# First batch's activation: the raw first 256 columns kept two places further on, and split without copies

## The chip, the cores and the metric

The kernel runs on one core of a Trainium2 chip. A core has a matmul engine (TensorE; PE in the rows, its weight loads PEld), a vector engine (VectorE, DVE), a scalar engine (ScalarE, ACT), a general engine (GpSimd, POOL) and a queue that issues transfers (SyncE, SP). The metric is device time in microseconds (us) of one execution of the whole program; the time given for the kernel is the median of its runs.

## The reference

```python
B, H, S, D = 4, 12, 448, 64          # batches, heads, tokens, head size
q_n, k_n = rmsnorm(q, g_q), rmsnorm(k, g_k)
attn = softmax(q_n @ k_n.T / 8)       # per head
x = (attn @ v)                        # heads side by side: 1792 tokens x 768
h = x @ moe_w_in                      # 768 -> 2048
g = h / (1 + exp(-1.702 * h))
y = g @ moe_w_out                     # 2048 -> 768
h2 = y @ moe2_w_in                    # 768 -> 2048
out = (max(h2, 0) + alpha * min(h2, 0)) @ moe2_w_out
```

All is float32. The weights and the four batches of tokens are needed whole; no step depends on the order in which batches are done.

## The kernel before

TensorE multiplies float16 here. So each float32 operand is split in two float16 parts, a high one (`hi`, made by ScalarE) and a low one (`lo`, what is left, made by VectorE as `scalar_tensor_tensor` from the float32 source and `hi`): `split`, lines 137 to 142, whose two instructions show as L139 and L140. A product is three matmuls (hi·hi, hi·lo, lo·hi).

**The stages.** Attention of batch 0 runs first, beside the unpacking of the two weight matrices of the first MoE layer. Its second half is interleaved with the first 256 token columns of batch 0's first matmul, because these are ready before the other 192. Then batch 0's remaining 192 columns, its activation and its second matmul (`first_moe1`, `moe1_out`) run beside the attention of batch 1; `moe1(b)` of the later batches runs beside the attention of the batch after it; and the second MoE layer ends the kernel.

**The first layer of batch 0.** There are KF = 16 blocks of 128 hidden units, m = 0 to 15. For each block `first_in(cols, m, g, t)` issues 18 matmuls into a PSUM tile `hp` (profile line L720), then a tanh on ScalarE into an SBUF tile `t` (L731), then `(tanh + 1) * hp` on VectorE (L732). It is called twice for a block: with columns 0 to 255 during the attention of batch 0, and with columns 256 to 447 in `first_moe1`. PSUM tiles `hp` come from `ps_m`, which has three buffers; `t` comes from the pool `work`, tag "t", which has two, and it is the same tag that `split_g`, `moe1` and the output `y` use.

**Where the result lies.** The tile `g0` has 16 places, one for each block, each of 2 x 448 float16: room for the two parts of the block, or for 448 float32 words. In its first half a place that isn't split yet keeps the block's float32 result ("raw"). `unsplit(g, m)` is place m seen as float32. The first 256 words of each place hold the raw first columns; the remaining 192 words of the 16 places are the landing area of the second weight matrix (`raw1o`), until it is unpacked.

**How it is split before the change.** Both parts of block m go to place m, where its raw result lies as well, so that the raw words have to be out of the way first. For blocks 0 to 4 (RAW0 = 5) the last 192 columns are written raw beside the first 256, and then, once the scales of the second weight matrix are known, `split_g` copies each block's 448 words to a `t` tile (L809) and splits from there. For blocks 5 to 15 a `t` tile is taken first, the 256 raw words are copied into it (L751), `first_in` puts the other 192 columns beside them, and the split reads that tile:

```python
t = work.tile([128, S], F32, tag="t", name="t")
nc.vector.tensor_copy(out=t[:, 0:FIRST], in_=unsplit(g, m)[:, 0:FIRST])
first_in(slice(FIRST, S), m, g, t)
split((g[:, m, 0], g[:, m, 1]), t, scales["w1o"][1][:, m:m + 1])
```

**What sets the order.** Each engine works its instructions in a fixed order. That order is not the program's: a planner runs through the program with costs of its own and puts on each engine what is ready, earlier program text first. A pool tile is given out in program order, so that a later user of `work` "t" waits until both uses of an earlier one are over. In program text the attention of batch 1 (`other_batches`) is interleaved with `first_moe1` and `moe1_out` by ticks; `B1_AT = 24` ticks pass before its first unit, that is 12 blocks. A unit of the attention of batches 1 to 3 is: scores (L499, PSUM pool `ps_s`, two buffers), maximum (L504, DVE), exponent (L523, ACT), reciprocal and a high part (L562, L565), a low part (L592, DVE), a transposing DMA (L598, SP), and the product with v (L616). `normalize` and `prep_pair` ready q and k of a pair of heads (L395, L397, L417, L418, L451, L452; for some pairs L417, L418 and L452 run on POOL). `v_scale(b)` loads v of a batch in pieces to the tiles `vst` of `raw_p` (two buffers) and reduces them (L310, L311).

Of the kernel before, what the change touches and what calls it, by code (L numbers as in the profile page):

```python
# [9 lines left out]
F32 = mybir.dt.float32  # L10
# [4 lines left out]
ALU = mybir.AluOpType  # L15
# [5 lines left out]
RAW0 = 5  # L21
# [35 lines left out]
def attention_moe_kernel(  # L57
# [17 lines left out]
    nc = tc.nc  # L75
# [7 lines left out]
    KF = FF // 128  # L83
# [7 lines left out]
    work = ctx.enter_context(tc.tile_pool(name="work", bufs=2))  # L91
# [45 lines left out]
    def split(dst, src, scale):  # L137

        nc.scalar.activation(out=dst[0], in_=src, func=AF.Copy, scale=scale)  # L139
        nc.vector.scalar_tensor_tensor(  # L140
            out=dst[1], in0=src, scalar=scale, in1=dst[0], op0=ALU.mult, op1=ALU.subtract
        )
# [111 lines left out]
    def later_rows(w, d, other):  # L254

        nj = w.shape[1]
        return lambda j: w[:, j + d].rearrange("p e n -> p (e n)").bitcast(F32) if j + d < nj else other(j)

    scales = {}
    loads = {}  # L260
    w1i = big.tile([128, KD, 2, FF], F16, tag="w", name="w1i", bufs=2)
    w1o = big.tile([128, KF, 2, DM], F16, tag="w", name="w1o", bufs=2)
# [3 lines left out]
    raw_p = att.enter_context(tc.tile_pool(name="raw_p", bufs=2))  # L266
# [206 lines left out]
    FIRST = 256  # L473
# [236 lines left out]
    def urgent(on):  # L710
        return tc.high_priority(on) if on else ExitStack()

    def first_in(cols, m, g, t):

        n = cols.stop - cols.start
        ps = ps_m.tile([128, n], F32, tag="m", name="hp")
        i = 0
        for kk in range(KD):
            for e, f in ((0, 0), (0, 1), (1, 0)):
                nc.tensor.matmul(  # L720
                    out=ps, lhsT=w1i[:, kk, e, m * 128:(m + 1) * 128], rhs=xs[0, kk][:, f, cols], start=(i == 0),
                    stop=(i == 3 * KD - 1)
                )
                i += 1
        if t is None:
            t = work.tile([128, S], F32, tag="t", name="t")
            dst = unsplit(g, m)
        else:
            dst = t
        with urgent(HP0):  # L730
            nc.scalar.activation(out=t[:, cols], in_=ps, func=AF.Tanh, scale=c_t[:, 0:1])  # L731
            nc.vector.scalar_tensor_tensor(out=dst[:, cols], in0=t[:, cols], scalar=1.0, in1=ps, op0=ALU.add, op1=ALU.mult)  # L732

    def moe1_scales(b):
        nc.vector.tensor_scalar(
# [4 lines left out]
    def first_moe1(g):  # L740

        for m in range(KF):
            if m == RAW0:
                for _ in w1o_steps:
                    pass
                split_g(g, scales["w1o"][1], range(RAW0))
            if m < RAW0:
                first_in(slice(FIRST, S), m, g, None)
            else:
                t = work.tile([128, S], F32, tag="t", name="t")  # L750
                nc.vector.tensor_copy(out=t[:, 0:FIRST], in_=unsplit(g, m)[:, 0:FIRST])  # L751
                first_in(slice(FIRST, S), m, g, t)
                split((g[:, m, 0], g[:, m, 1]), t, scales["w1o"][1][:, m:m + 1])
            yield
            yield
        yield from moe1_out(0, g)
# [24 lines left out]
    def moe1_out(b, g):  # L781
        nc.vector.tensor_scalar(
            out=c_y[:, b:b + 1], in0=c_y[:, b:b + 1], scalar1=scales["w1o"][0], scalar2=2.0 ** 11, op0=ALU.mult, op1=ALU.mult
        )
        for j in range(KD):
            ps = ps_m.tile([128, S], F32, tag="m", name="yp")
            n = 0
            for m in range(KF):
                for e, f in ((0, 0), (0, 1), (1, 0)):
                    nc.tensor.matmul(  # L790
                        out=ps, lhsT=w1o[:, m, e, j * 128:(j + 1) * 128], rhs=g[:, m, f], start=(n == 0), stop=(n == 3 * KF - 1)
                    )
                    n += 1
                if m in (3, 7, 11):
                    yield
            y = work.tile([128, S], F32, tag="t", name="y")
            with urgent(HP2):
                nc.scalar.activation(out=y, in_=ps, func=AF.Copy, scale=c_y[:, b:b + 1])
            nc.sync.dma_start(out=y_dram[j * 128:(j + 1) * 128, b * S:(b + 1) * S], in_=y)
            yield  # L800

    def unsplit(g, m):

        return g[:, m].rearrange("p e t -> p (e t)").bitcast(F32)

    def split_g(g, sc, ms=range(KF)):
        for m in ms:
            t = work.tile([128, g.shape[3]], F32, tag="t", name="t")
            nc.vector.tensor_copy(out=t, in_=unsplit(g, m))  # L809
            split((g[:, m, 0], g[:, m, 1]), t, sc[:, m:m + 1])  # L810

    TICKS = 2 * KF + 4 * KD

# [330 lines left out]
    if True:  # L1144
# [18 lines left out]
        def num1o(j):  # L1163
# [8 lines left out]
        w1o_steps = weights(  # L1172
            moe_w_out, "w1o", lambda: w1o, later_rows(w1o, 2, num1o), lambda t: raw1o[:, 4 * (t % R1O):4 * (t % R1O) + 4], 2,
            R1O, 2.0 ** -25, scales, G1O
        )
# [21 lines left out]
        for i, _ in enumerate(steps):  # L1197
            pairs = max(0, (i - LAG + 1) // 2)
            rows = KF - 2 if pairs >= 4 else (HOLD + pairs * HELD) // (2 * DM) - 2
            while n1o < min(1 + 2 * rows + 3 * (rows // 2), (i + 1) * W1O_RATE, 57):  # L1200
                next(w1o_steps)
                n1o += 1
            if i >= M_AT and i - M_AT < KF:
                first_in(slice(0, FIRST), i - M_AT, g0, None)
            if i == VS_AT:
                with tc.issue_after(loads["w1i"][-1].ins):
                    v_scale(1)
# [15 lines left out]
        for b in range(B):  # L1223
            last = min(NU, 4 * NP * (b + 2)) + LAG
            first = done
            got = None
            for i, _ in enumerate(moe1(b) if b else first_moe1(g0)):
                lead = 0 if b else B1_AT
                want = first + (last - first) * min(1.0, max(0.0, i + 1 - lead) / (PACE[b] * TICKS - lead))
                while done < min(want, NU + LAG):  # L1230
                    next(att_steps)
                    done += 1
                if b == B - 1:
                    for _ in range(1 if i < 2 * KF else 2):
                        if got is None or i >= 2 * KF:
                            got = next(late, None)
# [31 lines left out]
```

## Time and profile before

| | |
|---|---|
| median of 3 runs | 1184.49 us (1184.01 to 1185.91) |
| profiled execution | 1184.74 us |
| its span | 1183.0 us |
| PE busy | 1073.3 us, 91% of the span |
| DVE busy | 819.6 us, 69% |
| ACT busy | 673.3 us, 57% |
| POOL busy | 79.7 us, 7% |

The span runs from the first to the last instruction of the profile; the profiled execution's own time is 1.7 us more. Busy shares are averages over the whole program, and the stages differ. The stage that the change touches lies between about 122 and 258 us of the span. A granted clock of 1.00 is the upper of TensorE's two levels (2.4 GHz), 0.50 the lower one (1.2 GHz); a figure between is a stretch that had both.

### The profile page before, as it was taken

To read this page: it belongs to the slowest core of one execution; us is meant where nothing else is said; L and a number is where in the kernel's file an instruction comes from. 1 tells how busy PE (TensorE), PEld (TensorE's weight loads), DVE (VectorE), ACT (ScalarE), POOL (GpSimd) and SP (SyncE) were. 2 spreads that over 40 slices of the span, in tenths; PEclk is the share of its full clock that TensorE was granted. 3 is DMA by queue.
4 is the path that set the end of the run, shared out by engine and by line. 5 is a ranking of instruction groups with operands and counts; after the bars stand their busy time and mean duration, and the time that the engine had idled before them with its cause. 6 is when DMAs were issued, how large, how long until landed. Compare 5 with 4: busy or idle time off the path is not lost.

```text
span 1183.0 us, 18327 instructions
## 1 busy us (share of the span) xinstructions
PE 1073.3 (91%) x6755; PEld 586.6 (50%) x6755; DVE 819.6 (69%) x1445; ACT 673.3 (57%) x1348; POOL 79.7 (7%) x200
## 2 busy tenths in 40 slices
PE   3468799688789989999998999999999999999998
PEld 1234467554344444545454545544444467666665
DVE  6989999986767886467741868489996322978351
ACT  4667776787767875578742545256555423655220
POOL 2300001442011101100000000000000000000000
PEclk9579799899999999999998999999999999999999
DMA  7944542569888685666553821275624423353111
GB/s 232 266 144 137 150 135 77 113 138 182 160 158 157 136 157 121 122 122 115 93 128 65 307 92 52 99 255 178 224 78 144 142 72 123 99 173 101 34 30 31
DMA packets 256458, 158.06 MB, mean 134 GB/s; under 512 B 177648, under 2 KB 239728, under 8 KB 256368
## 3 DMA queue, kind: packets, MB, share of 16 engines
q1 hardware_dynamic: 256368, 156.89, 50.9%
q8 instruction: 53, 0.87, 0.3%
q14 instruction: 37, 0.30, 0.1%
HBM read 92.22 MB, written 25.69 MB: 100 GB/s over the span
## 4 chain that ended last, share of the span: by engine, by line
PE 32%; DVE 20%; DMA 10%; ACT 10%; issue 5%; SPq 3%; POOL 2%; ACTq 0%; POOLq 0%; DVEq 0%
PE op L1052 16%; PE h L892 7%; PE yp L790 5%; ACT pr L523 3%; DVE ph L592 3%; PE hp L767 3%; DVE nm L504 2%; ACT ph L565 2%; SPq L598 2%; DMA yr<-y_dram 2%; DMA qk<-in_q_dram 1%; DMA pt<-ph 1%; DMA t<-hl 1%; DVE g L140 1%; DMA vst<-in_v_dram 1%
## 5 line engine op out<-in xcount | busy, mean ns | idle before, releaser
L790 PE MATMUL yp<-g,w1o 128*128 128x448 f16 x1152 | 228.2, 355 | 1.9 <-DVE g L140 1.6
L892 PE MATMUL h<-x,w2i 128*128 128x512 f16 (+1 forms) x1152 | 218.9, 352 | 2.7 <-DVE pos L898 1.7
L767 PE MATMUL hp<-x,w1i 128*128 128x448 f16 x864 | 172.1, 356 | 3.7 <-DVE t L776 1.8
L892 PEld LDWEIGHTS <-w2i 128*128 128x128 f16 x1152 | 112.6, 98 | 108.1 <-issue 3.5
L790 PEld LDWEIGHTS <-w1o 128*128 128x128 f16 x1152 | 109.8, 98 | 111.8 <-issue 13.2
L767 PEld LDWEIGHTS <-w1i 128*128 128x128 f16 x864 | 82.8, 99 | 88.2 <-issue 15.7
L592 DVE SCALAR_TENSOR_TENSOR ph<-pr,sm,ph 128x448 f16<-128x448 f32 x126 | 86.9, 717 | 20.2 <-ACT ph L565 19.3
L504 DVE TENSOR_REDUCE nm<-sp 128x2 f32<-128x896 f32 x96 | 92.4, 963 | 0.4 <-PE sp L499 0.4
L523 ACT ACTIVATE pr<-sp,nm,c_s 128x448 f32<-128x448 f32 x126 | 90.0, 717 | 2.8 <-DVE ph L592 1.0
L897 ACT ACTIVATE pos<-h,sign 128x512 f32<-128x512 f32 (+1 forms) x64 | 40.2, 629 | 86.0 <-PE h L892 80.2
L565 ACT ACTIVATE ph<-pr,sm 128x448 f16<-128x448 f32 x126 | 77.8, 659 | 18.3 <-DVE sm L562 15.3
L1052 PEld LDWEIGHTS <-even 128*128 128x128 f16 x672 | 65.7, 98 | 43.4
L898 DVE SCALAR_TENSOR_TENSOR pos<-h,slope,pos 128x512 f32<-128x512 f32 (+1 forms) x64 | 43.4, 680 | 57.9 <-ACT pos L897 57.9
L720 PE MATMUL hp<-x,w1i 128*128 128x256 f16 (+1 forms) x576 | 63.9, 273 | 10.0 <-DVE t L732 4.8
L499 PE MATMUL sp<-t 64*128 64x448 f16 (+1 forms) x432 | 56.2, 365 | 17.0 <-ACT pr L523 17.0
L1052 PEld LDWEIGHTS <-odd 128*128 128x128 f16 x504 | 49.3, 98 | 32.6
L616 PE MATMUL xp<-pt,vs 128*64 128x256 f16 (+1 forms) x792 | 50.2, 271 | 16.6 <-DMA pt<-ph 8.4
L1052 PE MATMUL op<-w2lo,even 128*128 128x384 f16 x384 | 63.4, 326 | 0.0
L720 PEld LDWEIGHTS <-w1i 128*128 128x128 f16 x576 | 54.6, 103 | 17.5 <-issue 12.9
L140 DVE SCALAR_TENSOR_TENSOR g<-t,ratio_w1o,g 128x448 f16<-128x448 f32 x64 | 47.0, 736 | 15.0 <-ACT g L139 14.9
L506 ACT ACTIVATE nm<-nm,c_s 128x2 f32<-128x2 f32 x72 | 20.9, 290 | 62.4 <-DVE nm L504 62.2
L616 PEld LDWEIGHTS <-vs 128*64 128x64 f16 x792 | 39.3, 114 | 33.7 <-issue 18.7
(228 smaller groups left out, 1553.8 us busy)
## 6 DMA issues: line engine op xcount, KB each, us to landing
g<-in_moe_w_in_dram SPq DMA_DIRECT2D x24, 512.0 KB, 5.7
g<-in_moe_w_out_dram SPq DMA_DIRECT2D x32, 384.0 KB, 3.7
w2raw<-in_moe_w_in_dram SPq DMA_DIRECT2D x24, 512.0 KB, 5.6
w2raw<-in_moe_w_out_dram SPq DMA_DIRECT2D x16, 768.0 KB, 6.3
g_dram<-pos SPq DMA_DIRECT2D x48, 256.0 KB, 2.0
gp<-g_dram SPq DMA_DIRECT2D x8, 1024.0 KB, 6.7
odd<-g_dram SPq DMA_DIRECT2D x6, 1024.0 KB, 5.4
y_dram<-y SPq DMA_DIRECT2D x24, 224.0 KB, 2.5
```

The costliest lines, as they stand in the source:

```text
L140: nc.vector.scalar_tensor_tensor(out=dst[1], in0=src, scalar=scale, in1=dst[0], op0=ALU.mult, op1=ALU.subtract)
L499: nc.tensor.matmul(out=sp[:, j, 0:S] if n == 2 else sp[ds, 0, 0:S], lhsT=qt[ds] if n == 2 else qt[ds, 64:128], rhs=kt[ds, 0:S], start=(i = ...
L504: nc.vector.tensor_reduce(out=nm[:, 0:n], in_=sp[:, 0:n, 0:S], op=ALU.max, axis=AX, negate=True)
L523: nc.scalar.activation(out=pr[i], in_=sp[:, i, 0:S], func=AF.Exp, bias=nm[:, i:i + 1], scale=c_s if u >= 4 * NP else 1.0, accum_out=sm[:, ...
L565: nc.scalar.activation(out=ph[:, i, 0:S], in_=pr[i], func=AF.Copy, scale=sm[:, i:i + 1])
L592: nc.vector.scalar_tensor_tensor(out=ph[:, i, S:2 * S], in0=pr[i], scalar=sm[:, i:i + 1], in1=ph[:, i, 0:S], op0=ALU.mult, op1=ALU.subtract)
L616: nc.tensor.matmul(out=xp[64 * j:64 * j + 64, t:t + n], lhsT=vs[ks, j, c], rhs=pt[ks, kc, o:o + n], start=(i == 0), stop=(i == len(steps) ...
L720: nc.tensor.matmul(out=ps, lhsT=w1i[:, kk, e, m * 128:(m + 1) * 128], rhs=xs[0, kk][:, f, cols], start=(i == 0), stop=(i == 3 * KD - 1))
L767: nc.tensor.matmul(out=ps, lhsT=w1i[:, kk, e, m * 128:(m + 1) * 128], rhs=x[:, f], start=(n == 0), stop=(n == 3 * KD - 1))
L790: nc.tensor.matmul(out=ps, lhsT=w1o[:, m, e, j * 128:(j + 1) * 128], rhs=g[:, m, f], start=(n == 0), stop=(n == 3 * KF - 1))
L892: nc.tensor.matmul(out=ps, lhsT=w2i[:, kk, e, m * 128:(m + 1) * 128], rhs=x2[kk][:, f], start=(c == 0), stop=(c == 3 * KD - 1))
L1052: nc.tensor.matmul(out=ps, lhsT=ops[:, o, m, f], rhs=rhs[:, e], start=(c == 0), stop=(c == 3 * KH - 1))
```

## The change

The raw result of block m goes to place m + 2 of `g0` instead of place m. So place m is free, or its words have been read by the split of block m - 2, when block m is split, and the split reads the raw words where they lie. Blocks 14 and 15 have no place two further on: their 256 columns go to tiles of the tag "vst" of `raw_p`, and for these two the copy to `t` stays. Blocks 5 to 13 take no `t` tile for the split any more; their last 192 columns are written raw, like those of blocks 0 to 4 before. `first_in` still takes a `t` tile for the tanh.

```diff
@@ first_in
+        dst = raw_t(g, m)[:, cols] if t is None else t[:, cols]
         if t is None:
             t = work.tile([128, S], F32, tag="t", name="t")
-            dst = unsplit(g, m)
-        else:
-            dst = t
         with urgent(HP0):
             nc.scalar.activation(out=t[:, cols], in_=ps, func=AF.Tanh, scale=c_t[:, 0:1])
-            nc.vector.scalar_tensor_tensor(out=dst[:, cols], in0=t[:, cols], scalar=1.0, in1=ps, op0=ALU.add, op1=ALU.mult)
+            nc.vector.scalar_tensor_tensor(out=dst, in0=t[:, cols], scalar=1.0, in1=ps, op0=ALU.add, op1=ALU.mult)
@@ first_moe1
         for m in range(KF):
-            if m == RAW0:
-                for _ in w1o_steps:
-                    pass
-                split_g(g, scales["w1o"][1], range(RAW0))
-            if m < RAW0:
+            if m < KF - 2:
                 first_in(slice(FIRST, S), m, g, None)
             else:
                 t = work.tile([128, S], F32, tag="t", name="t")
-                nc.vector.tensor_copy(out=t[:, 0:FIRST], in_=unsplit(g, m)[:, 0:FIRST])
+                nc.vector.tensor_copy(out=t[:, 0:FIRST], in_=raw_t(g, m))
                 first_in(slice(FIRST, S), m, g, t)
-                split((g[:, m, 0], g[:, m, 1]), t, scales["w1o"][1][:, m:m + 1])
+            if m == RAW0 - 1:
+                for _ in w1o_steps:
+                    pass
+                split_g(g, range(RAW0))
+            elif m >= RAW0:
+                split_g(g, (m,), t if m >= KF - 2 else None)
@@ helpers
-    def unsplit(g, m):
-
-        return g[:, m].rearrange("p e t -> p (e t)").bitcast(F32)
-
-    def split_g(g, sc, ms=range(KF)):
+    last_t = {}
+
+    def raw_t(g, m):
+
+        if m < KF - 2:
+            return g[:, m + 2].rearrange("p e t -> p (e t)").bitcast(F32)
+        if m not in last_t:
+            last_t[m] = raw_p.tile([128, FIRST], F32, tag="vst", name="last_t")
+        return last_t[m]
+
+    def split_g(g, ms, t=None):
         for m in ms:
-            t = work.tile([128, g.shape[3]], F32, tag="t", name="t")
-            nc.vector.tensor_copy(out=t, in_=unsplit(g, m))
-            split((g[:, m, 0], g[:, m, 1]), t, sc[:, m:m + 1])
+            split((g[:, m, 0], g[:, m, 1]), raw_t(g, m) if t is None else t, scales["w1o"][1][:, m:m + 1])
```

## Rows read from the trace of the kernel before

**Rows 1.** the page's first part: engine, busy us, share of span, count

```profile
PE 1073.3 (91%) x6755; PEld 586.6 (50%) x6755; DVE 819.6 (69%) x1445; ACT 673.3 (57%) x1348; POOL 79.7 (7%) x200
```

**Rows 2.** windows, 206 to 250 us: length; busy PE, PEld, DVE, ACT, POOL; clock; DMA; GB/s

```profile
206.00:212.00 6.00, 6.00 (x73) 5.24 (x70) 4.37 (x16) 2.60 (x4) 0.00 (x0) 1.00 0.88 190
212.00:220.00 8.00, 1.60 (x11) 0.58 (x8) 8.00 (x14) 6.58 (x16) 2.96 (x4) 0.83 0.61 142
220.00:230.00 10.00, 7.39 (x49) 5.96 (x48) 9.12 (x15) 9.25 (x24) 9.02 (x16) 0.67 0.25 48
230.00:240.00 10.00, 8.47 (x90) 6.28 (x88) 9.89 (x18) 7.82 (x20) 2.58 (x3) 0.96 0.78 143
240.00:250.00 10.00, 8.23 (x93) 6.37 (x93) 8.52 (x20) 9.02 (x24) 4.16 (x5) 1.00 0.72 161
```

**Rows 3.** TensorE's timeline, 206 to 243 us: start, us, instruction, idle before, releaser

```profile
206.35 4.62 PE L720 MATMUL hp<-x,w1i 128*128 128x192 f16 x54
210.90 1.31 PE L499 MATMUL sp<-t 64*128 64x448 f16 x12
217.93 1.30 PE L499 MATMUL sp<-t 64*128 64x448 f16 x6 [5.72 <-ACT pr L523]
219.91 3.04 PE L720 MATMUL hp<-x,w1i 128*128 128x192 f16 x18 [0.68 <-DVE t L732]
...
226.81 4.78 PE L720 MATMUL hp<-x,w1i 128*128 128x192 f16 x36 [2.61 <-DVE t L732]
...
240.57 3.13 PE L720 MATMUL hp<-x,w1i 128*128 128x192 f16 x36 [1.48 <-DVE t L732]
```

**Rows 4.** the copies: L809 by its instructions (ns min/median/max), L751 as a group

```profile
L809 DVE COPY t<-g x5: 375/384/393, 206.3 to 218.5; 128x448 f32<-128x448 f32 x5
L751 DVE COPY t<-g 128x256 f32<-128x256 f32 x11 | 4.7, 431 | 0.0
```

**Rows 5.** VectorE's timeline: copies and low parts

```profile
210.18 0.69 DVE L809 COPY t<-g 128x448 f32<-128x448 f32 x2
...
222.60 1.27 DVE L751 COPY t<-g 128x256 f32<-128x256 f32 x1
...
230.73 2.89 DVE L140 SCALAR_TENSOR_TENSOR g<-t,ratio_w1o,g 128x448 f16<-128x448 f32 x2
...
247.48 0.87 DVE L751 COPY t<-g 128x256 f32<-128x256 f32 x1
```

**Rows 6.** GpSimd's timeline at the same times

```profile
222.46 1.27 POOL L417 TENSOR_TENSOR qk<-qk,gs 128x512 f32<-128x512 f32 x1
...
230.52 2.03 POOL L452 TENSOR_TENSOR hl<-qk,hl 128x896 f16<-128x896 f32 x1 [0.20 <-ACT hl L451]
...
246.92 1.27 POOL L417 TENSOR_TENSOR qk<-qk,gs 128x512 f32<-128x512 f32 x1 [4.92 <-ACT sq L395]
```

**Rows 7.** chain of waits, 212 to 250 us: start, us, what

```profile
222.69 1.19 DVE t L751
...
225.07 0.24 DVE t L751
...
242.78 2.99 DMA qk<-in_q_dram
...
247.56 0.79 DVE t L751
```

**Rows 8.** ScalarE's timeline: the tanh of blocks 5 and 8

```profile
217.77 0.41 ACT L731 ACTIVATE t<-hp,c_t 128x192 f32<-128x192 f32 x1
...
233.06 0.42 ACT L731 ACTIVATE t<-hp,c_t 128x192 f32<-128x192 f32 x1 [1.91 <-DVE g L140]
```

**Rows 9.** windows after 260 us, the same columns

```profile
260.00:460.00 200.00, 176.66 (x1243) 87.72 (x1241) 151.76 (x271) 146.26 (x343) 26.19 (x72) 0.97 0.78 153
460.00:600.00 140.00, 137.95 (x940) 69.00 (x937) 85.43 (x144) 98.86 (x231) 3.66 (x14) 0.99 0.63 114
```

**Rows 10.** SyncE's timeline: the next loads to the tiles vst

```profile
285.83 0.92 SPq L310 DMA_DIRECT2D vst<-in_v_dram  x2
```

## The prediction

> **What bounds the kernel now.** The page's first part comes first: TensorE is busy 91% of the span, VectorE 69% [rows 1]. That average says that the kernel is a matmul kernel; it doesn't say what holds the stage of the change. The table of busy time by stretch does. From 212 to 250 us TensorE works 1.60 of 8, 7.39 of 10, 8.47 of 10 and 8.23 of 10 us, VectorE 8.00, 9.12, 9.89 and 8.52 [rows 2]. So VectorE is the engine that is never free there (35.53 of 38 us, 93%), and ScalarE follows with 32.67 of 38 (86%). TensorE waits: its timeline has one gap of 5.72 us before the third group of scores, and gaps of 0.68, 2.61 and 1.48 us in which `hp` matmuls wait for VectorE's L732 to empty a PSUM tile [rows 3]. The reader is to see in the same rows that the granted clock falls after the first gap, to 0.83 and then 0.67 in the stretches [rows 2], and that 18 `hp` matmuls then take 3.04 us, while 54 had taken 4.62, or 1.54 for 18 [rows 3].
>
> The chain of waits, cut to 212 to 250 us, names what of this reaches the end: it has VectorE, ScalarE and transfer pieces, and no matmul. Three of the copies that the change removes are pieces of it, with 1.19, 0.24 and 0.79 us, 2.22 us together; so are transfers, the longest a load of q that takes 2.99 us [rows 7]. After 260 us TensorE is busy 176.66 of 200 us, so 23.3 us of idle time are left there, and from 460 us on it has next to none (137.95 of 140) [rows 9].
>
> **The change part by part.** *Copies.* Of 16 copies 14 go. The five of line 809 have a median of 0.384 us, 1.92 us in all; the eleven of line 751 take 4.7 us, of which nine go [rows 4]. Two of the nine took 1.27 and 0.87 us [rows 5], so that the other nine of the eleven are (4.7 - 1.27 - 0.87) / 9 = 0.28 us each; the nine that go are 4.7 - 2 x 0.28 = 4.1 us. VectorE loses 6.0 us of work. Four copies of line 809 lie before 212 us (two of them at 210.18 [rows 5]), in a stretch where VectorE is busy 4.37 of 6 us [rows 2]: these 1.5 us are hidden behind its own idle time, and I put them at nothing; if that idle time were gone they would be 1.5 us of gain. The other ten, 4.5 us, lie in the stretch that VectorE fills. The upper bound is therefore 4.5 us, if each microsecond counts. The chain says 2.2.
>
> *What the long copies were long of.* The copy at 222.60 ends at 223.87, when GpSimd's operation of 222.46 (1.27 us) has ended; the one at 247.48 ends at 248.35, behind GpSimd's of 246.92 (to 248.19) [rows 5, 6]. Two low parts, which read two tiles of SBUF, took 2.89 us at 230.73 beside GpSimd's 2.03 us from 230.52 [rows 5, 6]. So the stretch of 0.99 and 0.59 us is a wait for GpSimd, and the next instruction of VectorE may inherit it. Without it the three chain pieces shrink to about 0.28 + 0.24 + 0.28 = 0.8 us, my lower bound. I take 1.5, midway to the chain's 2.2: after one of the long copies a low part comes next, after the other a reduction.
>
> The Trainium skill, page "SBUF — State Buffer", section "SBUF: two separate sides", gives a rule that speaks against the change here: VectorE and GpSimd share a pair of ports under an exclusive lock, a VectorE operation with two SBUF inputs takes part in it as a two-port copy does, and the loser is blocked until the other is done. By that rule the low part, which has two SBUF inputs, waits in the copy's place, and the first term is 0.8 and not 1.5. The trace agrees as far as the low parts at 230.73 go; which instruction will stand there after the change no row can tell.
>
> *The `t` tiles.* Before, a `t` tile was held from the copy to the end of the split; now, for blocks up to 13, only from the tanh to L732. The 54 `hp` matmuls from 206.35 (blocks 5 to 7, 18 each) are done by 210.97, but the tanh of block 5 runs at 217.77; block 8's starts at 233.06 after ScalarE has stood idle 1.91 us for a low part to give its tile back [rows 3, 8]. That wait stands at the head of ScalarE's queue, and the high parts and exponents of attention stand behind it. It goes: 1.9 us. Its lower bound is 0, if VectorE, itself held by GpSimd then, sets the pace there; the upper one adds TensorE's three gaps for L732, 4.8 us, 6.7 in all. I take 1.9, since the gaps of TensorE are not in the chain.
>
> *What is added.* The raw words of block m go to place m + 2. Their L732 has the same size as before. A split's high part now has to wait for the low part of two blocks earlier, which reads the place that it writes; before it waited as long for its `t` tile, of which there are two. So the depth is the same, and I put it at 0; ends -0.9 and +0.9, what the two low parts at 230.73 took beyond GpSimd's 2.03 [rows 5, 6]. The tiles "vst" are idle: the next loads to them start at 285.83 [rows 10], 38 us behind the copy at 247.48, the ninth of eleven and so block 13's; only two more follow. Cost 0; if one of these came after that load's turn, SP's queue with the transposes behind it would stand still.
>
> *Sum.* 1.5 + 1.9 = 3.4 us less. Attention goes on behind this stage in instructions that follow one another, and TensorE has 23.3 us of idle time before 460 us to give up [rows 9], so I let it pass through in full: 1184.74 - 3.4 = 1181.3. The profiled execution lies 0.25 us above the median of the runs shown, which changes nothing at this size.
>
> **The rivals.** *The stretch stays.* VectorE waits for GpSimd in another instruction: 0.8 + 1.9 = 2.7, 1182.0. For it: the low parts of 230.73; against it: the planner may put an operation with one SBUF source there. The page's rule named above says the same.
>
> *TensorE is let go.* With `t` free, `hp` matmuls fill the gap of 5.72 us and the three of 4.77, and the clock stays up: the 18, 36 and 6 matmuls at a lowered clock cost 3.04 - 1.54, 4.78 - 3.08 and about half of 1.30 us more, 3.9 us [rows 3]. If half of these 14.4 us passes, beside the copies, 7.2 + 1.5 = 8.7: 1176.0; all would be 1168.8. For it: VectorE's lines are what each gap ended on but one; against: no matmul is in the chain.
>
> *Absorbed.* Transfers set the pace: the load at 242.78 of 2.99 us, in the chain [rows 7], starts when it can, and work before it that ends earlier waits. Then only the third copy, behind that load, is saved, at most 0.79: 1184.0 to 1184.7, say 1184.4. For it: a DMA share of 0.72 to 0.78 from 230 us [rows 2]; against: the loads wait for tiles that VectorE and ScalarE free.
>
> *Slower: the scores of batch 1 go back.* These start at 210.90 because `hp` matmuls are stuck for `t` and PSUM tiles [rows 3]. Freed, the eight blocks 8 to 15, earlier in program text, may be put ahead of them: 8 x 1.54 = 12.3 us later. The gap of 5.72 us is then no loss, and 2.2 us of copies are gone: 12.3 - 5.7 - 2.2 = 4.4 later for an attention that sets the pace until 460 us: 1189.1. It decides if the first scores of batch 1 start later than about 219 us (210.9 plus what is saved). For it: the planner takes earlier text first; against: it also fills gaps, and `hp` still has only three PSUM tiles.
>
> **How the numbers follow.** A change under 0.2%, 2.4 us, can hardly be told from none: faster is below 1182.1, slower above 1186.9. Chances: forecast 0.37 (its own range 1178.5 to 1183.5, 0.07 of it within 0.2%), the stretch stays 0.10 (half within), TensorE let go 0.15, absorbed 0.18, slower 0.20. Faster 0.30 + 0.05 + 0.15 = 0.50, same 0.07 + 0.05 + 0.18 = 0.30, slower 0.20. The range leaves out the further half of the large gain and the worst third of the slower case: 1174.0 to 1189.5.
>
> **What would show it.** In the profile after: no copies but two at 256 columns; the tanh of block 5 near 211 us, not 217.77; no wait of ScalarE's L731 for a low part; VectorE's busy time about 6 us less in all. Right, if the second matmul of batch 0 (L790) begins some 3 us earlier and TensorE's idle time from 260 to 460 doesn't grow. Wrong, if the first scores of batch 1 come after 219, if long low parts take the copies' place in full, or if idle time after 260 us grows by what was won.

## The result, and the profile after

The changed kernel takes 1195.13 us (median of 5 runs, 1194.97 to 1195.99), the kernel before 1185.91 in the runs taken beside it (1184.01 to 1186.95): a ratio of 1.0086, with a 95% interval of 1.0074 to 1.0098. It is 9.2 us slower. Forecast were 1181.3 us, 3.4 us less than the profiled execution of before: the sign is wrong, and the time lies above the range. The profiled execution of after took 1195.99 us, its span 1194.2.

The page's first part, engine, busy us, share, count:

```profile
PE 1076.9 (90%) x6755; PEld 588.3 (49%) x6755; DVE 811.5 (68%) x1431; ACT 671.6 (56%) x1348; POOL 79.9 (7%) x200
```

VectorE has 14 instructions and 8.1 us of work less than in [rows 1]. So the change does what it says. The stretches (length; busy PE, PEld, DVE, ACT, POOL; clock; DMA; GB/s), first those of [rows 2], then later ones:

```profile
206.00:212.00 6.00, 6.00 (x57) 5.85 (x55) 3.58 (x13) 2.46 (x5) 0.00 (x0) 0.74 0.86 169
212.00:220.00 8.00, 7.80 (x89) 6.31 (x87) 7.84 (x14) 7.97 (x21) 2.96 (x3) 1.00 0.68 164
220.00:230.00 10.00, 7.52 (x86) 6.80 (x85) 9.75 (x19) 9.28 (x25) 8.77 (x17) 1.00 0.24 46
230.00:240.00 10.00, 4.23 (x26) 2.01 (x25) 10.00 (x16) 8.06 (x20) 3.82 (x2) 0.82 0.48 81
240.00:250.00 10.00, 10.00 (x64) 4.83 (x63) 4.95 (x10) 5.78 (x14) 2.85 (x2) 0.84 0.72 135
...
260.00:460.00 200.00, 163.81 (x1135) 82.13 (x1134) 141.30 (x255) 140.18 (x332) 26.09 (x70) 0.92 0.75 148
300.00:340.00 40.00, 23.02 (x170) 11.99 (x170) 31.62 (x59) 29.09 (x73) 4.58 (x14) 0.70 0.88 179
460.00:600.00 140.00, 139.98 (x959) 70.60 (x959) 86.93 (x146) 96.51 (x224) 4.41 (x18) 0.98 0.65 117
```

The kernel before, the one stretch of these that was not shown:

```profile
300.00:340.00 40.00, 33.67 (x261) 17.00 (x261) 25.52 (x53) 27.07 (x68) 0.00 (x0) 0.96 0.78 154
```

In the stage of the change TensorE is better off (7.80 of 8 us busy in 212 to 220, before 1.60). The loss is later. From 260 to 460 it is busy 12.9 us less than in [rows 9], and 10.65 of these belong to 300 to 340, where the clock is down as well, 0.70 for 0.96. TensorE's timeline of after, first around the change and then around the loss (start, us, instruction, idle before, releaser):

```profile
208.35 4.97 PE L720 MATMUL hp<-x,w1i 128*128 128x192 f16 x54
213.25 1.31 PE L499 MATMUL sp<-t 64*128 64x448 f16 x12
214.50 4.63 PE L720 MATMUL hp<-x,w1i 128*128 128x192 f16 x54
...
237.95 7.10 PE L789 MATMUL yp<-g,w1o 128*128 128x448 f16 x23
...
302.09 1.69 PE L789 MATMUL yp<-g,w1o 128*128 128x448 f16 x8
304.02 0.75 PE L499 MATMUL sp<-t 64*64 64x448 f16 x6 [0.24 <-ACT pr L523]
...
313.01 1.30 PE L499 MATMUL sp<-t 64*128 64x448 f16 x6 [2.22 <-ACT pr L523]
...
329.26 1.30 PE L499 MATMUL sp<-t 64*128 64x448 f16 x6 [5.54 <-DMA t<-hl]
...
336.69 0.23 PE L119 MATMUL pm<-diag,ones 128*128 128x128 bf16 x1
336.76 8.49 PE L789 MATMUL yp<-g,w1o 128*128 128x448 f16 x44
```

The same place in the kernel before:

```profile
314.37 0.74 PE L499 MATMUL sp<-t 64*128 64x448 f16 x6
...
321.39 0.27 PE L119 MATMUL pm<-diag,ones 128*128 128x128 bf16 x1 [0.51 <-DVE diag L117]
321.45 7.76 PE L790 MATMUL yp<-g,w1o 128*128 128x448 f16 x36
```

The first layer runs ahead as in the rival "TensorE is let go": the 54 `hp` matmuls at 214.50 follow on the scores at once, the gap of 5.72 us of [rows 3] is gone, and the second matmul of batch 0 (L790 before, L789 now) starts at 237.95 instead of 249.19, 11.2 us earlier. But its first four output blocks (192 matmuls) are done by 303.8, and the fifth starts at 336.76. Between them no `yp` matmul runs, and what does run, scores and products with v, waits for ScalarE and transfers. What the fifth block stands behind is one matmul of L119, called `pm`: it takes the maximum over the partitions for the scale of v of batch 2 (`partition_max`, called by `v_scale(2)`). `pm` and `yp` take their tiles from the same PSUM pool, `ps_m`, tag "m", whose tiles are given out in program order. Program text has `v_scale(2)` between the fourth and the fifth block. Before, the four blocks were done at 314.4 and `pm` came at 321.39, so the wait was 7 us; now it is 33.

Why `pm` is later although `yp` is earlier shows first of all on SyncE, which issues the loads of v that this maximum is taken of. The row for line 598 counts the transposes (`pt`) ahead of the first load of L310 (min/median/max ns, first and last start). Kernel before, which loads at 285.83 [rows 10]:

```profile
L598 SPq DMA_TRANSPOSE pt<-ph x24: 1190/1254/1997, 225.1 to 283.9; - x24
```

Changed kernel, and then its loads in SyncE's timeline:

```profile
L598 SPq DMA_TRANSPOSE pt<-ph x34: 1207/1248/1712, 225.9 to 308.8; - x34
```

```profile
310.12 1.05 SPq L310 DMA_DIRECT2D vst<-in_v_dram  x2
315.74 1.00 SPq L310 DMA_DIRECT2D vst<-in_v_dram  x2
320.50 1.01 SPq L310 DMA_DIRECT2D vst<-in_v_dram  x2
326.41 1.71 SPq L310 DMA_DIRECT2D vst<-in_v_dram  x2
```

The planner has put the loads of v behind ten more transposes: the first is issued at 310.12, 24 us later. They come in four pairs, since `vst` has two tiles. The fourth pair, without which the maximum can't be taken, is 12.4 us later, because before the change 19 us lay between the second pair and the third. Before, the fourth pair was

```profile
313.98 1.01 SPq L310 DMA_DIRECT2D vst<-in_v_dram  x2
```

`pm` is 15.3 us later; the other 3 us lie on VectorE, which takes 5.5 us from the last reduction of v to the operand of `pm` (330.73 to 336.24), before 2.5 (318.57 to 321.09). The chain of waits of after, 296 to 340 us (start, us, what), follows them to the gate (the place where later work is held up):

```profile
310.12 3.04 DMA vst<-in_v_dram
...
313.19 0.98 DVE vcol L311 x2
...
326.41 3.29 DMA vst<-in_v_dram
...
330.73 0.49 DVE vcol L311
...
336.01 0.74 PE sp L499 x6
336.76 0.16 PE pm L119
```

Counting the score matmuls of batches 1 to 3 in both traces: after's 145th starts at 329 us, 4 us ahead of before; its 181st at 377, 11 us behind; the last starts at 630.6 instead of 618.7. So nearly all is lost between 329 and 377, while TensorE makes up for the output blocks that were held up. TensorE has less to do from 440 to 460, too, around batch 3's maximum: 14.79 us busy, before 19.45. That this is a second gate isn't shown: its `pm` runs at 448.67, but the longest idle stretch, 3.01 us up to 458.16, ends on a high part of ScalarE (and `pm` of before, at 438.57, lies outside these 20 us).

### The profile page after: what moved, and what is told of

It is laid out like the page before. It is cut to its first block, busy times and chain, and to the rows that moved or that the text cites. A ratio compares the mean times of both kernels' runs of the same rounds, so it can differ in the third digit from the quotient of the medians.

```text
span 1194.2 us, 18311 instructions
## 1 busy us (share of the span) xinstructions
PE 1076.9 (90%) x6755; PEld 588.3 (49%) x6755; DVE 811.5 (68%) x1431; ACT 671.6 (56%) x1348; POOL 79.9 (7%) x200
## 4 chain that ended last, share of the span: by engine, by line
PE 47%; DVE 13%; DMA 8%; ACT 7%; issue 4%; SPq 3%; POOL 1%; ACTq 0%; DVEq 0%
PE op L1055 16%; PE yp L789 12%; PE h L895 10%; PE hp L766 6%; ACT pr L523 2%; DVE nm L504 2%; PE xp L616 2%; DVE ph L592 2%; SPq L598 1%; DMA w2raw<-in_moe_w_in_dram 1%; PE sp L499 1%; DMA qk<-in_q_dram 1%; ACT ph L565 1%; DMA t<-hl 1%; DVE w2num L164 1%
## 5 line engine op out<-in xcount | busy, mean ns | idle before, releaser
L789 PE MATMUL yp<-g,w1o 128*128 128x448 f16 x1152 | 230.7, 359 | 4.2 <-ACT g L139 3.0
L766 PE MATMUL hp<-x,w1i 128*128 128x448 f16 x864 | 169.3, 353 | 6.2 <-DVE x L140 3.1
L789 PEld LDWEIGHTS <-w1o 128*128 128x128 f16 x1152 | 111.4, 99 | 117.0 <-issue 19.7
L592 DVE SCALAR_TENSOR_TENSOR ph<-pr,sm,ph 128x448 f16<-128x448 f32 x126 | 83.8, 691 | 23.5 <-ACT ph L565 23.3
L616 PE MATMUL xp<-pt,vs 128*64 128x256 f16 (+1 forms) x792 | 53.3, 283 | 20.8 <-DMA pt<-ph 15.5
L397 DVE TENSOR_REDUCE ss<-sq 128x7 f32<-128x448 f32 x48 | 28.2, 613 | 32.0 <-ACT sq L395 32.0
```

Source lines behind the costliest of these rows:

```text
L592: nc.vector.scalar_tensor_tensor(out=ph[:, i, S:2 * S], in0=pr[i], scalar=sm[:, i:i + 1], in1=ph[:, i, 0:S], op0=ALU.mult, op1=ALU.subtract)
L616: nc.tensor.matmul(out=xp[64 * j:64 * j + 64, t:t + n], lhsT=vs[ks, j, c], rhs=pt[ks, kc, o:o + n], start=(i == 0), stop=(i == len(steps) ...
L766: nc.tensor.matmul(out=ps, lhsT=w1i[:, kk, e, m * 128:(m + 1) * 128], rhs=x[:, f], start=(n == 0), stop=(n == 3 * KD - 1))
L789: nc.tensor.matmul(out=ps, lhsT=w1o[:, m, e, j * 128:(j + 1) * 128], rhs=g[:, m, f], start=(n == 0), stop=(n == 3 * KF - 1))
```

## Experiments

Each was run beside the kernel before on the same chip (medians 1185.6 to 1186.4); ratios are to that. Theory 1 is that the late maximum of v costs the time, and the change itself does not; the rival, theory 2, is that the first layer runs ahead of attention and puts it back. There are NP = 6 pairs of heads to a batch, P counts them over the batches, and `v_scale(2)` stands in the text at P = 2 NP - 2, step r = 2.

**e1: the maximum one pair earlier, in the changed kernel.**

```diff
-if r == 2 and P % NP == NP - 2 and P // NP + 1 < B:
+if (P, r) in ((2 * NP - 3, 2), (3 * NP - 2, 2)):
```

> The changed kernel with one edit: the loads and the maximum of batch 2's v stand one pair of heads earlier in the program text. Theory 1 (the late maximum): the changed kernel loses because the fifth output block of batch 0 waits for the PSUM tile of that maximum, which comes at 336.7 us of its span and at 321.4 before the change; its TensorE is idle 17.0 of 40 us between 300 and 340, against 6.3 before. Put earlier, the maximum lies before the fourth block and the wait goes: 1182 to 1187 us. Theory 2 (attention put back): the last 192 columns of the first layer run ahead of batch 1's scores, which are 8 us later at the 72nd matmul, and that delay is the loss; the place of the maximum changes nothing: 1194 to 1196.

Measured: 1195.59 us, 1.0094 [1.0068, 1.0119]. This is not what I expected; it lies in the range of theory 2. The loads came 18 us earlier, but `pm` moved forward in the text as well, ahead of the fourth block, and ran at 317.92. So the gate had only moved by a block: no `yp` matmul ran from 286 to 318.

**e2: the maximum two steps later, in the kernel before.**

```diff
-if r == 2 and P % NP == NP - 2 and P // NP + 1 < B:
+if (P, r) in ((2 * NP - 1, 0), (3 * NP - 2, 2)):
```

> The kernel before with one edit: the loads and the maximum of batch 2's v stand two units of attention later in the text, so that the maximum's matmul comes behind 178 score matmuls as in the changed kernel, and not behind 154; copies and places are those of before. Theory 1: the loss appears without the change: 1193 to 1198 us. Theory 2: nothing has moved in the first layer: 1184 to 1187.

Measured: 1194.42 us, 1.0081 [1.005, 1.0112]. The loss appears without anything of the change, as theory 1 had it. In its trace 162 score matmuls of batches 1 to 3 lie ahead of `pm`, as in the changed kernel, for 138 before (the counts in the expectation are 16 higher, the step of 24 is the same). TensorE in 300 to 340 and around the gate:

```profile
300.00:340.00 40.00, 27.70 (x181) 13.21 (x181) 26.37 (x51) 27.84 (x72) 0.00 (x0) 0.66 0.83 168
```

```profile
339.74 0.23 PE L119 MATMUL pm<-diag,ones 128*128 128x128 bf16 x1
339.80 5.46 PE L790 MATMUL yp<-g,w1o 128*128 128x448 f16 x28
```

**e3 and e4: batch 2's maximum by a transfer and back** (the helpers that the kernel has for this), so that it takes no PSUM tile; e3 in the changed kernel, e4 in the one before.

```diff
-partition_max(mv[:, b:b + 1], one)
+if b == 2:
+    take_max(mv[:, b:b + 1], send_max(one))
+else:
+    partition_max(mv[:, b:b + 1], one)
```

> The changed kernel with one edit: the maximum of batch 2's v over the partitions is taken by a round trip through memory and not by a matmul into a PSUM tile. The loads stay as late as in the changed kernel. Theory 1 in the form that the PSUM tile is what the fifth block waits for: 1183 to 1188 us. If instead the lateness of batch 2's scale itself (the v of batch 2 is split with it) is what costs, 1193 to 1197. Theory 2: 1194 to 1196.

> The kernel before with the same one edit as the run ahead of it. Control: it tells what the round trip is worth by itself. Theory 1: the smaller wait of before, from 314.4 to 321.4 us, goes too: 1180 to 1186 us. Theory 2: 1184 to 1187.

Measured: 1190.69 us (1.0051 [1.0025, 1.0077]) and 1191.06 us (1.0055 [1.0035, 1.0074]). Both miss what either theory gave: the detour, with the order that the planner makes of it, costs some 5 us of its own. But between the two nothing is left of the 9.2 us (some 0.3% either way), although the loads still stand behind 34 transposes in e3 and 24 in e4, and TensorE is busy 30.62 and 31.78 of 40 us in 300 to 340.

**e5 and e6: batch 2's loads two pairs earlier, its maximum where it was**; e5 changed, e6 before.

```diff
-v_scale(P // NP + 1)                      # at P = 2 NP - 2
+v_scale(2, 1)                             # the maximum alone
...
+if (P, r) == (2 * NP - 4, 2):
+    with tc.issue_after(moved[P].ins):
+        v_scale(2, 0)                     # loads and reductions (L310, L311)
```

> The changed kernel with one edit: the loads of batch 2's v and the maximum of each piece stand two pairs of heads earlier in the text; the maximum over the partitions, with its PSUM tile, stays at its place. Theory 1 (the PSUM gate): what costs is that the fifth output block of batch 0 gets its PSUM tile only behind this maximum, and the maximum is late because its loads are. The run ahead with the whole step earlier kept the gate and moved it to the fourth block (matmul of the maximum at 317.9 us, no output matmul from 286 to 318). With the loads alone earlier the maximum is ready when block 4 runs: no gap over 5 us in the output matmuls, and 1181 to 1187 us. Theory 2 (the filler is used up): TensorE's work that doesn't depend on attention begins 11 us sooner and is gone 11 us sooner, so that TensorE waits for attention anyway, as in the run with the maximum by memory (1190.7): 1189 to 1195.

> The kernel before with the same edit as the run ahead of it. Control: the gap of before, 314.4 to 321.4 us, should close too. Theory 1: 1180 to 1186 us. Theory 2 says nothing of it, 1184 to 1187 as a no-change.

Measured: e5 1184.14 us, 0.9992 [0.9973, 1.0011]: as expected, the loss is gone, though one idle stretch of 6.9 us in the output matmuls (321.0 to 327.9) is left where none over 5 was expected. e6 1188.84 us, 1.0022 [1.0008, 1.0037]: not expected, a little slower than before. In e5 the gate lies inside the work:

```profile
290.97 0.36 PE L802 MATMUL yp<-g,w1o 128*128 128x448 f16 x1
291.17 0.22 PE L119 MATMUL pm<-diag,ones 128*128 128x128 bf16 x1
291.23 1.30 PE L802 MATMUL yp<-g,w1o 128*128 128x448 f16 x6
```

**e7 and e8: parts of the change.** e7 keeps the new places and puts the fourteen copies back, with `t` held as before; e8 is the changed kernel with the tanh's `t` of blocks 5 to 13 held until after the split, by a copy of one column.

For e7, blocks 5 to 15 (and likewise the 448 words of blocks 0 to 4 in `split_g`):

```diff
+t = work.tile([128, S], F32, tag="t", name="t")
+nc.vector.tensor_copy(out=t[:, 0:FIRST], in_=raw_t(g, m)[:, 0:FIRST])
-split_g(g, (m,), t if m >= KF - 2 else None)
+split_g(g, (m,), t)
```

For e8, after the split of blocks 5 to 13:

```diff
+nc.vector.tensor_copy(out=got, in_=tanhs[m][:, FIRST:FIRST + 1])
```

> The changed kernel with the 14 copies put back: the raw words stay two places further on and blocks 14 and 15 in the other tiles, but each block is copied to a t tile, which is held until it is split, as before. Theory 1: places and tiles cost nothing, the matmul of the maximum stands behind 148 score matmuls (154 before, 178 in the changed kernel): 1182 to 1188 us. If the new places or the shared tiles were the cause: 1193 to 1196.

> The changed kernel, still without copies, but each tanh tile of blocks 5 to 13 is held until its block is split (a copy of one column reads it there, 0.1 us each). If the early release of t is what lets the first layer run ahead and so what moves the maximum: 1183 to 1188 us. Theory 1 with the order that the planner gives here (outputs begin after 46 score matmuls, as in the changed kernel; maximum behind 166): between, 1188 to 1196.

Measured: e7 1193.1 us, 1.0068 [1.0051, 1.0085], a miss, and inside what the rival gave: the kernel with the new places loses time although the copies are there. It isn't batch 2's gate that does it (`pm` at 322.84, TensorE 33.71 of 40 us busy in 300 to 340). e8 1197.65 us, 1.0112 [1.0091, 1.0133], above both of what was expected: that `t` is let go earlier isn't the cause; TensorE is as idle in 300 to 340 as in the changed kernel (23.45 us busy).

The two also tell what moves the loads of v. In e8 34 transposes lie ahead of the first load, as in the changed kernel, and it is issued at 312.29. In e7 there are 22, and the first load is

```profile
283.65 1.05 SPq L310 DMA_DIRECT2D vst<-in_v_dram  x2
```

So the loads go back with the copies that are gone. It is neither the new places, nor the early release of `t` alone, nor that blocks 14 and 15 share the "vst" tiles, since e7 has both the places and these tiles. Why the planner decides so is not shown.

**e9 and e10: the loads of batches 2 and 3 both two pairs earlier**; e9 changed, e10 before. **e11 and e12: e7 with batch 2's loads earlier, and with both.** The edit is that of e5, for e9, e10 and e12 also at P = 3 NP - 4 for batch 3.

> The changed kernel with the loads of v of batches 2 and 3, both, two pairs of heads earlier and the maxima over the partitions where they were. If what is left over in the changed kernel with batch 2's loads earlier (1184.1) is a wait for batch 3's maximum (TensorE 17.0 us busy in 440 to 460, against 19.45 before the change), the time is 1180 to 1183.5, with 18.5 us or more busy in that stretch. If that idle time is only TensorE running dry after having been ahead, moving the loads gives nothing: 1183.5 to 1186, and the idle time comes back elsewhere.

> The control: the same two edits in the kernel before the change. First theory (the change is worth its 3.4 us wherever the maxima don't stand in the way): 3 to 5 us above the changed kernel with the same edits, 1184 to 1188.5. If the change is worth nothing by itself and the earlier loads had won it: the same time as that one within 1.5 us.

> The changed kernel with its places two further on, but with the fourteen copies put back and batch 2's loads of v two pairs earlier. If the places cost nothing by themselves and only the order of the loads and copies counts: as the kernel before with the same loads, 1188.8, that is 1186.5 to 1190.5. If the places cost time by themselves, as the kernel with places alone (1193.1) let one think: 1192 to 1197.

> Places two further on, the fourteen copies put back, and the loads of v of batches 2 and 3 both two pairs earlier. If the two maxima account for what this kernel lost with batch 2's loads alone earlier (1189.9), it comes to the two others with both earlier (1183.1 and 1183.6): 1182 to 1186, with 18 us or more of TensorE busy in 440 to 460 (16.4 with batch 2's alone). If the places cost by themselves, because the first layer's raw columns wait longer, it stays at 1188 to 1191.

Measured: e9 1183.14 us (0.9983 [0.997, 0.9995]) and e10 1183.62 us (0.9982 [0.9969, 0.9995]): both are 0.2% faster than the kernel before, and they are equal. e9 is as expected (20.00 us busy in 440 to 460); for the control the theory's range fell, and the other case that I had named, the same time within 1.5 us, is what came. e11 1189.93 us, 1.0042 [1.0026, 1.0058], in the range that I had given if the places cost nothing; e12 1189.95 us, 1.003 [1.002, 1.004], not the theory's range: it stays where I had put it if the places cost by themselves, although 440 to 460 is full (19.98 us). TensorE in e9, then e10, in 206 to 250 and 260 to 460:

```profile
206.00:250.00 44.00, 33.50 (x304) 25.03 (x303) 35.90 (x66) 31.69 (x75) 17.42 (x21) 0.88 0.56 112
260.00:460.00 200.00, 176.48 (x1230) 86.59 (x1230) 152.43 (x271) 148.58 (x351) 30.80 (x74) 0.97 0.79 155
```

```profile
206.00:250.00 44.00, 31.01 (x292) 23.09 (x290) 38.77 (x74) 36.33 (x88) 19.41 (x26) 0.84 0.63 129
260.00:460.00 200.00, 178.16 (x1246) 88.33 (x1246) 149.77 (x271) 147.14 (x350) 26.64 (x71) 0.97 0.79 152
```

Of the 2.49 us that TensorE works more in the first stretch 1.68 come back as less work in the second. What the places cost stands ahead of both, where the raw first columns are written and the second weight matrix is unpacked. The windows of e10 and, of the fourteen low parts of that matrix that VectorE makes in place, the last eight (L179; min/median/max ns, first and last start), then the same of e12:

```profile
160.00:180.00 20.00, 19.32 (x155) 13.14 (x157) 18.73 (x50) 17.06 (x40) 0.00 (x0) 1.00 0.62 165
180.00:206.00 26.00, 24.15 (x247) 20.97 (x248) 23.84 (x54) 15.28 (x31) 4.17 (x14) 1.00 0.19 48
```

```profile
L179 DVE SCALAR_TENSOR_TENSOR w1o<-w1o,inv_w1o x8: 1001/1010/1021, 156.3 to 186.8; 128x768 f16<-128x768 f32 x8
```

```profile
160.00:180.00 20.00, 17.48 (x147) 12.08 (x145) 17.57 (x46) 14.13 (x37) 0.00 (x0) 1.00 0.50 138
180.00:206.00 26.00, 22.37 (x219) 18.61 (x218) 23.12 (x49) 16.74 (x32) 4.20 (x14) 1.00 0.25 60
```

```profile
L179 DVE SCALAR_TENSOR_TENSOR w1o<-w1o,inv_w1o x8: 1005/1011/1019, 155.9 to 192.3; 128x768 f16<-128x768 f32 x8
```

The last of them starts 5.5 us later with the new places (192.3 for 186.8; 2.7 us later in the changed kernel than in the one before, 191.1 for 188.4), and TensorE does 3.6 us less in 160 to 206 (39.85 us for 43.47). The `pm` of that matrix, L119 again, comes at 208.72 for 204.68 and the first scores at 214.4 for 209.5. It is so in every kernel with the new places (`pm` at 208.2 to 210.2) and in none with the old ones (206.3 or earlier). Only e3 and e4, whose first `pm` comes 5 us earlier than in the others, lie lower, with 204.28 and 197.94, and there the new places are later as well.

**e13: batch 3's loads alone earlier, in the changed kernel.** The edit of e5 for P = 3 NP - 4 and batch 3 only.

> The changed kernel with batch 3's loads of v alone two pairs earlier; batch 2's stay where they were. If batch 2's maximum is the main loss (its loads alone brought 1195.1 to 1184.1, and batch 3's on top of that 1.0): 1192 to 1195, with the stage 300 to 340 as empty as in the changed kernel (23.0 of 40 us busy). If the idle time at 440 to 460 is a loss of its own of 4 to 5 us: 1189 to 1191.

Measured: 1199.7 us, 1.0112 [1.0098, 1.0126]. Neither time came: 300 to 340 is as idle as expected (21.91 us busy, the changed kernel 23.02) and 440 to 460 is full (20.00), yet it is slower than the changed kernel by 0.26% (1.0112 to 1.0086). That 440 to 460 is filled gains nothing while the gate of batch 2 stands.

## Why the prediction was wrong

*Copies (1.5 us taken, bounds 0.8 and 4.5).* VectorE's 8.1 us less were a little more than the 6.0 worked out. Between kernels that differ in the copies and in how long `t` is held, with the loads out of the way, it is worth 1.0042 to 0.9992 (e11 to e5) and 1.003 to 0.9983 (e12 to e9): 0.5% in both, 5.6 to 5.9 us, for both terms together, which I had at 3.4. So on top of the new places these two were of the right sign and too small.

*The t tiles (1.9 us).* Right in place. ScalarE's timeline has the tanh of block 5 at 211.09, not 217.77 [rows 8]:

```profile
211.09 0.40 ACT L729 ACTIVATE t<-hp,c_t 128x192 f32<-128x192 f32 x1
```

No tanh waits for a low part any more, and TensorE's waits for VectorE in `hp` are 0.40, 0.36 and 1.92 us for the 0.68, 2.61 and 1.48 of [rows 3]. Locally it came as the rival "TensorE is let go" had it, and a new gap of 5.77 us at 232 to 237.6, which ends on a transposing transfer, didn't take it back.

*GpSimd.* As the rival "the stretch stays" had it, other instructions inherit the wait. VectorE, then GpSimd:

```profile
228.08 1.84 DVE L140 SCALAR_TENSOR_TENSOR g<-g,ratio_w1o 128x448 f16<-128x448 f32 x1
229.84 1.77 DVE L745 COPY t<-last_t 128x256 f32<-128x256 f32 x1
```

```profile
227.74 3.72 POOL L418 TENSOR_TENSOR qk<-qk,rs 128x896 f32<-128x896 f32 x2
```

A low part takes 1.84 us where others take 0.67, and one of the two copies left 1.77 for 0.28, both beside GpSimd's 3.72, which end at 231.46, the copy at 231.61. This is the Trainium skill's rule, page "SBUF — State Buffer", section "SBUF: two separate sides", that the two engines lock each other out of their shared ports; the trace agrees. It costs VectorE 2.7 us here and isn't what decided.

*What is added (0, ends -0.9 and +0.9).* Mis-sized. I looked for the cost in the splits and in the "vst" tiles after 206 us. But the raw columns are written between 126 and 200 us, beside the unpacking of the second weight matrix, whose words land in the same 16 places, and there the order came out otherwise. The new places with the copies kept cost 1.003 to 0.9982, 0.48% or 5.7 us (e12 to e10), 0.2% with only batch 2's loads earlier (e11 to e6; from both intervals, 0 to 0.4%), and 0.68% with the loads where they were (e7). The rows show that unpacking is later. Which of its waits does it, and whether the places themselves or the "vst" tiles of blocks 14 and 15 do, no run tells apart.

*The sum: "so I let it pass through in full".* This step failed. TensorE's 23.3 us of idle time from 260 to 460 us were taken as room that earlier work would fill. They grew to 36.2 us instead, which the prediction had named as a sign of being wrong. What ends an idle stretch there is set by something else: with the first layer ahead and the loads of v ten transposes further back, the gate of batch 2's maximum held the second matmul of batch 0 up for 33 us, in which TensorE had only attention, and that waited for ScalarE and transfers. The evidence: the loss arises without the change when that maximum is put later (e2, +0.81%); it goes when the loads are earlier (e5; 1.0086 to 0.9992, 0.94% or 11 us) or when the maximum takes no PSUM tile (e3 against e4); moving the gate with the loads does nothing (e1). With both loads out of the way the change is worth 0.01% (e9 against e10, some 0.2% either way); with batch 2's alone -0.3% (e5 against e6). A clean size for it doesn't come out of these runs: the controls change places with one another by as much as the effect. Nor is the gate the whole account. The 9.2 us are made of some 11 for the gate, up to 5.7 for the new places and 5.6 to 5.9 back for copies and `t`, which fits to within 2 us only, and e7 loses 0.68% with the gate's wait at 6 us (`yp` idle from 317.0 to 322.9); what costs that kernel its time stays open.

*The rivals.* The slower one named the scores of batch 1 going back, and a start after 219 us as the point from which it decides. They start at 213.25, so it was not that. I looked for work put back on TensorE; it is loads of a later batch that went back, on SyncE. Whether "the planner takes earlier text first" is the reason no run shows. [Rows 10] had these loads, at 285.83, and I read them only for whether the "vst" tiles are free, and not for who waits for the loads' result.

## What to carry to other kernels

When work is freed in a kernel whose order a planner makes, ask of each shared pool what the next tile in program order waits for: a small operation that looks unimportant (here one matmul of 0.23 us) can hold up the later users of its pool. Idle time of the matmul engine is room only if what ends it can come earlier; follow the releaser of each large gap back to its transfer before it is counted as a gain. And measure a change with its neighbours moved, too: the same edit was worth +0.86%, -0.3% and 0 with three placements of the loads of v.

## What was not expected of the hardware

TensorE's clock fell in the stretch of the gate. In 300 to 340 us it is granted 0.70, between its two levels, after gaps of 2 to 6 us; the same six scores take 1.30 us at 313.01 and at 329.26 and 0.74 at 301.42 and 336.01. So a gate can cost more than its idle time, since what runs between the gaps is slower, too; how much of the loss this is no run tells.
